# Linear attention, a softly gated mixture and a three-way max layer: banks from pools, the last layer's weights walked there and back, background work placed later

## The chip, the cores and the metric

One core of one Trainium2 chip runs the whole program in one launch. The metric is the device time of one execution in microseconds; the kernel before has a median of 1975.58 us over 3 runs (1972.33 to 1978.89).

## The reference

Three layers follow one another on 2304 tokens of 512 numbers. The first is attention with random features (4 batches, 8 heads, 576 tokens of 64). The second is a mixture of 8 experts, all of which see all tokens; its gate P is normalised by rows and columns eight times. The third takes the larger of three products and multiplies once more.

```
x   = attention(q, k, v, omega)                  # 2304 x 512
P   = exp(x @ w_gate - max); 8 times: P /= P.sum(1); P /= P.sum(0); P *= N / E
y   = sum over e of P[:, e] * (relu(x @ w1[e]) @ w2[e])      # 8 x (512 x 1024, 1024 x 512)
out = maximum(y @ m1, y @ m2, y @ m3) @ m_out                # 512 x 768 three times, 768 x 512
```

## The kernel before

**Tiles and stages.** The tokens are cut into three thirds of 768 and each layer is walked a third at a time, in phases 0 to 5. Phase 0 runs both layers of the mixture over the first third, phases 1 and 2 over the other two, and phases 3, 4 and 5 run the last layer over thirds one to three. A product of (768 tokens x 512) by (512 x 256) is computed by Winograd's scheme with seven products instead of eight. Its tokens' side is seven operands x0 to x6 (`x_operands`, stored in DRAM as xc1 to xc5 and loaded again by `load_x`), and its weights' side is seven operands made from w1 (`prepare_w1`) or from the last layer's weights (`last_weights`, stored as lc1 and lc2). Each number is split in a high and a low part, so that a product is six matmuls of 128x384 on PE (lines L401 to L403), all into one bank of the accumulator memory.

**A sub.** `sub_products` issues seven products into three kinds of banks: U (two banks in turn), V and W (one bank each). ACT copies U and V out as u1, u5 and u2 (L408), DVE adds them onto the other banks, and the four results go to ACT and DVE, which write h as a high part (ACT, L447 or L452) and a low part (DVE, L448 or L453). `tile_out` (L471 to L473) multiplies h by the second weights into one of four result banks, which DVE or ACT empties into acc (L484, L486). In phase 0 PE also runs one matmul for each of the eight gate rounds (L644), whose input cs DVE makes (L635 to L639 and L645 to L648); the gate begins with a maximum over all partitions on POOL (L630).

**The last layer.** A phase there has three turns of three subs. A sub's weights are seven pieces of 256 KB, loaded ahead into the tiles wa and wb in turn. The second weights of a turn are two pieces of 512 KB in w2_0 and w2_6 or w2_3 and w2_5. The seven operands of the next phase are loaded into x0 to x6 as their last readers in the phase before finish. The operands of phase 5 are computed in phase 3 into h0 to h5 and stored from there to xc5.

**What sets the order.** The attention is written out by hand. From there on, every step is a task with a cost, the keys that it reads and writes and the engines that may do it ("PD": POOL or DVE). `Tasks.ordered` (lines 41 to 149) plays the tasks through once: each engine takes, of the tasks that could start first, the one that is wanted earliest, and PE's tasks keep the order of the program. The instructions then stand on each engine in that order, and no engine passes over a waiting one. A load's time counts there as its bytes by a rate and a fixed part:

```python
return min(cost.values()) if on != "S" else 2000 + cost["S"]
```

All DMAs are issued by SP (`fetch`, L213), in one row, so a DMA whose tile is not yet free holds back those behind it. DVE and POOL additions go through one helper (`tt`, L210); so rows that read "L210" are of many places, and are told apart by their tiles. Names in the rows: g are raw weights or sums of them, w is w2_0 to w2_6, b is b11 to b22 and t is t1 to t4.

Of the kernel before, what the change touches and what calls it, by code (L numbers as in the profile page):

```python
# [23 lines left out]

FILL = 9
START = [("load", 0), ("squared", 0), ("squared", 1), ("norms", 0, 0), ("v", 1), ("load", 1), ("v", 0)]

# [13 lines left out]
class Tasks:  # L41
# [30 lines left out]
    def ordered(self):  # L72
# [24 lines left out]
        open_ = {e: set() for e in free}  # L97
        ready, port, wire = [0.0] * n, 0.0, 0.0
        best = dict.fromkeys(free)

        def choose(e):

            starts = []
            for i in open_[e]:
                t = max(free[e], ready[i])
                if e == "P" or e == "D" and tasks[i][4]:
                    t = max(t, port)
                starts.append((t, i))
            if not starts:
                return None  # L110
            t0 = min(starts)[0]
            return t0, min((wanted[i], i) for t, i in starts if t <= t0)[1], e
# [6 lines left out]
        for _ in range(n):  # L119
            for e in free:  # L120
                if best[e] is None:
                    best[e] = choose(e)
            start, i, e = min((b for b in best.values() if b), key=lambda b: (b[0], b[1]))
            order.append((i, e))
            for f in tasks[i][0]:
                open_[f].discard(i)
                best[f] = None
            cost = tasks[i][1][e]
            if e == "S":
                wire = max(wire, start) + cost  # L130
                free[e], end = start + 60, wire + 2000
            else:
                free[e] = start + cost
                end = free[e] + lag[e]
                if e == "P" or e == "D" and tasks[i][4]:
                    port = free[e]
                    best["P"] = best["D"] = None
            for j in after[i]:
                ready[j] = max(ready[j], free[e] if tasks[j][0] == e != "S" else end)
                left[j] -= 1  # L140
                if not left[j]:
                    for f in tasks[j][0]:
                        open_[f].add(j)
                        best[f] = None
# [4 lines left out]
def tile_performer__moe__max3(ctx, tc, kq_t, kq, v1, omega2, w_gate, w1, w2, m1, m2, m3, m_out, out):  # L149
# [49 lines left out]

    BANKS = [f"bank{k}" for k in range(8)]  # L200
    banks = {}

    def new_bank(k):
        return ps_m.tile([P, 512], F32, tag=k, name=k)

# [31 lines left out]
    def dma(kb, out, in_, r, w):  # L237
        return add("S", kb * 1024 / 350, lambda e: fetch(out(), in_()), r, w)

# [138 lines left out]
    u_turn = [0, 0, 1]  # L378
    U_BANKS, V_BANK, W_BANK = (BANKS[1], BANKS[0]), BANKS[2], BANKS[3]
    R_BANKS = BANKS[4:]  # L380
    r_turn = [0]

    def next_r():
        r_turn[0] += 1
        return R_BANKS[r_turn[0] % 4]

    def sub_products(k, before, results):

        ub = U_BANKS[u_turn.pop(0)]
        u_turn.append(1 - u_turn[-1])  # L390
        at = {"u": ub, "v": V_BANK, "w": W_BANK}

        def product(i, j, b, onto):
            before(i, j)
            kh, kl = w_keys(k, i)

            def run():
                ps, w, x = banks[b][:, :Q], ws[k][:, i].rearrange("p c (k f) -> p c k f", k=2), xo[j]
                given = dict(skip_group_check=onto)
                for c in range(2):  # L400
                    nc.tensor.matmul(ps, w[:, 0, c], x[:, c, 0], start=c == 0 and not onto, stop=False, **given)  # L401
                    nc.tensor.matmul(ps, w[:, 0, c], x[:, c, 1], start=False, stop=False, **given)  # L402
                    nc.tensor.matmul(ps, w[:, 1, c], x[:, c, 0], start=False, stop=c == 1, **given)  # L403

            pe(6 * 175, run, [*kh, *kl, (f"x{j}", 0), (f"x{j}", 1)], [b])

# [9 lines left out]
        to_u("u1", ub)  # L416
        product(*p[1], V_BANK, False)
        yield
        to_u("u5", V_BANK)
        product(*p[2], ub, True)  # L420
        yield
        to_u("u2", ub)
        product(*p[3], W_BANK, False)
        yield
        results(0, 0, W_BANK, lambda b, plus=plus: plus(W_BANK, W_BANK, "u1"), ("u1", W_BANK))
        product(*p[4], ub, True)
        yield
        results(1, 1, W_BANK, lambda b, plus=plus: plus(W_BANK, ub, "u5"), ("u5", ub))
        product(*p[5], V_BANK, True)
        yield  # L430
        results(0, 1, V_BANK, lambda b, plus=plus: plus(V_BANK, V_BANK, "u2"), ("u2", V_BANK))
        product(*p[6], ub, True)
# [122 lines left out]
    def h_parts(ks):  # L555
        return [(lambda k=k: t_(f"h{k}"), [(f"h{k}", 0)], [(f"h{k}", 1)]) for k in ks]

    def temps():
        return [(lambda k=k: t_(k), [k]) for k in ("b11", "b12", "b21", "b22", "t1", "t2")]
# [14 lines left out]

    def load_x(ph, j):
        for c in range(2):
            dma(384, lambda c=c: xo[j][:, c].bitcast(F32), lambda c=c: xc[ph][j][:, c], [("xc", ph, j, c)], [(f"x{j}", c)])

# [80 lines left out]
    def program():  # L659
# [19 lines left out]
        for s in range(SUBS):  # L679
# [175 lines left out]
        def max_results(m, parity):  # L855
# [17 lines left out]
            return results  # L873

        LAST = [("w2_0", "w2_6"), ("w2_3", "w2_5")]
        turn = 0
        for ph in (3, 4, 5):
            for n in range(3):
                parity = turn % 2
                tiles = LAST[parity]  # L880
                for m in range(3):
                    slot = (turn * 3 + m + 1) % 2

                    def before(i, j, n=n, m=m, slot=slot):
# [5 lines left out]
                    for i, _ in enumerate(sub_products(slot, before, max_results(m, parity))):  # L890
                        q = 7 * m + i
                        if len(queue) > 6:
                            take()
                        elif q >= 3 and q % 3 == 0 and not (ph == 3 and n == 0):
                            take()
                        elif ph == 3 and n == 0:
                            take()
# [8 lines left out]

                def weights(n=n, tiles=tiles):
                    for c, k in enumerate(tiles):
                        dma(512, lambda c=c, k=k: t_(k).bitcast(F32), lambda c=c: lc2[n][:, c], [("lc2", n)],
                            [(k, 0), (k, 1)])  # L910

                group = [lambda t=t, parity=parity, tiles=tiles, evict=evict: tile_out(t, parity, tiles, evict) for t in TILES]
                first = group[0]
                group[0] = lambda first=first, weights=weights: (weights(), first())
                queue += group
# [13 lines left out]
    def attention(pool, proj_pool):  # L929
# [3 lines left out]

        smalls.append(new_bank(BANKS[7]).rearrange("p (s j t h) -> p s j t h", s=2, j=2, t=128 // 2)[:, :, :, :TP])
        count = [0]
# [224 lines left out]
        def logits(s):  # L1160
# [10 lines left out]

            ps = new_bank(ring[(count[0] - 2) % 7]) if len(ring) == 7 else abank()
            for c in range(KD):
# [16 lines left out]
            def transposed():  # L1190
                ps = new_bank(ring[(count[0] - 2) % 7]) if len(ring) == 7 else abank()
                for j in range(n):
# [50 lines left out]

    smalls, ring = [], BANKS[:7]
    with tc.manual_schedule():
# [4 lines left out]
        with left as att:  # L1250
# [8 lines left out]
            ts.update({f"h{k}": a.tile([P, 2, Q], F32R, name=f"h{k}") for k in range(14)})  # L1259
            banks.update({k: new_bank(k) for k in BANKS[1:4]})  # L1260
            ring[:] = [BANKS[k] for k in (4, 5, 6, 0)]
            layers = feed_forward()
# [5 lines left out]
        while n < FILL:  # L1268
            next(layers)
            n += 1  # L1270
        banks.update({k: new_bank(k) for k in BANKS if k not in banks})
        b = ctx.enter_context(tc.tile_pool(name="b", bufs=1, side="left", reuse_waits="tile"))
# [62 lines left out]
```

## Time and profile before

| | |
|---|---|
| median of 3 runs | 1975.58 us (1972.33 to 1978.89) |
| the profiled execution | 1972.07 us, of which the span of the trace is 1970.1 |
| PE busy | 1888.4 us, 96% of the span |
| DVE, POOL, ACT busy | 75%, 50%, 40% |
| DMA | 579.49 MB, mean 294 GB/s |
| granted PE clock, mean of the span | 0.989 of full speed |

A row of a timeline begins with its start in us from the begin of the span and its duration; in square brackets stands the time for which its engine sat idle before it, and what ended that. "PEclk" is the granted clock as a share of the full one: 1.00 is 2.4 GHz and 0.50 is 1.2 GHz; a stretch with a value between holds some time at either. Phase 0 stands in the trace from about 196 us (its first products run beside the end of the attention), and phases 1 to 5 begin at about 735, 1190, 1690, 1754 and 1856 us.

### The profile page before, as it was taken

How to read it: one execution, taken by the hardware profiler on the slowest of the kernel's cores; microseconds unless marked ns; L12 is line 12 of the kernel's file. 1: busy time of each engine (PE TensorE's matmuls, PEld its weight loads, DVE VectorE, ACT ScalarE, POOL GpSimd, SP SyncE). 2: the span in 40 equal slices, each digit the busy share in tenths (PEclk: the TensorE clock that was granted, in tenths of full speed). 3: DMA queues.
4: the chain of work that ended last, by engine and by line, in shares of the span. 5: the costliest groups of instructions: out<-in, count | busy, mean ns of one | idle time of the engine just before them, and what ended most of it. 6: DMA issues, size and time to landing. Idle time of an engine off the chain costs nothing.

```text
span 1970.1 us, 33400 instructions
## 1 busy us (share of the span) xinstructions
PE 1888.4 (96%) x11521; PEld 1782.1 (90%) x11521; DVE 1481.7 (75%) x2694; ACT 796.4 (40%) x1805; POOL 984.9 (50%) x915
## 2 busy tenths in 40 slices
PE   7887899999999999999999999999999999989898
PEld 6666789878999999999999999999999999889897
DVE  6664798888878768988888888989886775633435
ACT  6665445545544435333333343433343332312221
POOL 4351577634455515686777775677764443300000
PEclk9999899999999999999999999999999999999999
DMA  6453789999988899899898898988998889987873
GB/s 213 159 151 131 273 279 386 372 347 332 339 317 300 315 341 352 328 330 316 316 312 311 307 335 285 319 316 294 312 387 290 259 249 352 355 314 218 301 236 117
DMA packets 282793, 579.49 MB, mean 294 GB/s; under 512 B 26528, under 2 KB 125568, under 8 KB 276992
## 3 DMA queue, kind: packets, MB, share of 16 engines
q1 hardware_dynamic: 282624, 577.35, 83.9%
q8 instruction: 92, 1.51, 0.3%
q14 instruction: 77, 0.63, 0.1%
HBM read 399.99 MB, written 177.26 MB: 293 GB/s over the span
## 4 chain that ended last, share of the span: by engine, by line
PE 85%; DVE 6%; DMA 4%; ACT 3%; issue 1%; POOL 1%; SPq 0%; DVEq 0%; POOLq 0%; ACTq 0%
PE bank L401 14%; PE bank L403 14%; PE bank L402 14%; PE bank L788 8%; PE bank L786 8%; PE bank L787 8%; PE bank L471 5%; PE bank L473 5%; PE bank L472 5%; PE bank L1023 2%; DMA x<-xc 2%; ACT qp L1046 1%; PE bank L956 1%; PE bank L1069 1%; ACT kp L1046 1%
## 5 line engine op out<-in xcount | busy, mean ns | idle before, releaser
L401 PE MATMUL bank<-x,wa 128*128 128x384 f32 x1302 | 441.1, 339 | 16.0 <-DVE bank L210 6.5
L403 PE MATMUL bank<-x,wa 128*128 128x384 f32 x1302 | 439.9, 338 | 9.5 <-DVE wa L210 9.5
L402 PE MATMUL bank<-x,wa 128*128 128x384 f32 x1302 | 438.7, 337 | 0.0
L408 ACT COPY u<-bank 128x384 f32<-128x384 f32 x369 | 176.9, 480 | 350.9 <-PE bank L403 348.0
L788 PE MATMUL bank<-h,w 128*128 128x384 f32 x896 | 303.2, 338 | 0.0
L786 PE MATMUL bank<-h,w 128*128 128x384 f32 x896 | 302.9, 338 | 0.0
L787 PE MATMUL bank<-h,w 128*128 128x384 f32 x896 | 301.9, 337 | 0.0
L210 DVE TENSOR_TENSOR acc<-bank,acc 128x384 f32<-128x384 f32 x420 | 231.4, 551 | 80.8 <-PE bank L788 79.4
L401 PEld LDWEIGHTS bank<-x,wa 128*128 128x128 f32 x1302 | 245.7, 189 | 27.2 <-DVE bank L210 7.6
L210 DVE TENSOR_TENSOR bank<-bank,u 128x384 f32<-128x384 f32 x342 | 191.9, 562 | 89.3 <-PE bank L403 83.2
L403 PEld LDWEIGHTS bank<-x,wa 128*128 128x128 f32 x1302 | 245.6, 189 | 11.4 <-DVE wa L210 11.1
L402 PEld LDWEIGHTS bank<-x,wa 128*128 128x128 f32 x1302 | 245.5, 189 | 5.0
L210 POOL TENSOR_TENSOR h<-b,h 128x384 fp32r<-128x384 f32 x144 | 155.7, 1090 | 143.4 <-ACT h L734 134.8
L210 POOL TENSOR_TENSOR h<-t,h 128x384 fp32r<-128x384 f32 x137 | 146.4, 1072 | 108.3 <-ACT h L734 94.3
L471 PE MATMUL bank<-w,h 128*128 128x512 f32 x492 | 195.2, 397 | 0.7 <-ACT h L452 0.7
L473 PE MATMUL bank<-w,h 128*128 128x512 f32 x492 | 194.5, 395 | 0.1
L472 PE MATMUL bank<-w,h 128*128 128x512 f32 x492 | 194.5, 395 | 0.0
L734 ACT CAST h<-b 128x384 fp32r<-128x384 f32 x192 | 98.3, 514 | 225.5 <-DVE b L749 208.5
L734 ACT CAST h<-t 128x384 fp32r<-128x384 f32 x256 | 127.5, 514 | 137.1 <-POOL t L210 109.6
L210 POOL TENSOR_TENSOR g<-g,g 128x256 f32<-128x256 f32 (+2 forms) x143 | 144.8, 1014 | 67.3 <-DVE g L210 30.7
L786 PEld LDWEIGHTS bank<-h,w 128*128 128x128 f32 x896 | 168.5, 188 | 0.0
L787 PEld LDWEIGHTS bank<-h,w 128*128 128x128 f32 x896 | 168.5, 188 | 0.0
(150 smaller groups left out, 3591.2 us busy)
## 6 DMA issues: line engine op xcount, KB each, us to landing
wa<-wc SPq DMA_DIRECT2D x441, 256.0 KB, 5.1
w<-wc SPq DMA_DIRECT2D x217, 512.0 KB, 5.7
g<-in_moe_w_dram SPq DMA_DIRECT2D x82, 512.0 KB, 7.4
wc<-w SPq DMA_DIRECT2D x64, 512.0 KB, 7.0
wc<-wa SPq DMA_DIRECT2D x16, 1792.0 KB, 8.6
wc<-wb SPq DMA_DIRECT2D x16, 1792.0 KB, 7.4
x<-xc SPq DMA_DIRECT2D x70, 384.0 KB, 7.5
wb<-lc SPq DMA_DIRECT2D x98, 256.0 KB, 4.7
```

The costliest lines, as they stand in the source:

```text
L210: (nc.gpsimd if on == "P" else nc.vector).tensor_tensor(out=out, in0=in0, in1=in1, op=op)
L401: nc.tensor.matmul(ps, w[:, 0, c], x[:, c, 0], start=c == 0 and not onto, stop=False, **given)
L402: nc.tensor.matmul(ps, w[:, 0, c], x[:, c, 1], start=False, stop=False, **given)
L403: nc.tensor.matmul(ps, w[:, 1, c], x[:, c, 0], start=False, stop=c == 1, **given)
L408: act(Q, lambda: nc.scalar.copy(t_(n), banks[b][:, :Q]), [b], [n])
L471: nc.tensor.matmul(ps, h[:, 0, c], t_(wh)[:, part], start=f == 0, stop=False)
L472: nc.tensor.matmul(ps, h[:, 0, c], t_(wl)[:, part], start=False, stop=False)
L473: nc.tensor.matmul(ps, h[:, 1, c], t_(wh)[:, part], start=False, stop=f == 1)
L734: act(Q, lambda: nc.scalar.copy(t_(h)[:, 0], t_(n)), [n], [(h, 0)])
L786: nc.tensor.matmul(ps, wv[:, 0, sub, d], h[:, 0], start=o == 0, stop=False)
L787: nc.tensor.matmul(ps, wv[:, 0, sub, d], h[:, 1], start=False, stop=False)
L788: nc.tensor.matmul(ps, wv[:, 1, sub, d], h[:, 0], start=False, stop=o == 1)
```

## The change

Five things change.

1. The accumulator's eight banks are taken from three pools, "ph" (4), "po" (3) and "small" (1), instead of by fixed numbers. When the attention ends, U0, V0 and W are the three of "po", U1, V1 and two result banks the four of "ph", and the third result bank is "small". So V has two banks, which take turns with U's, and results have three banks instead of four.
2. The planner counts a load as 3.5 us (instead of 2) beside its bytes, and its rate as 340 (instead of 350). DVE is not offered a task that POOL could do as well before 6 us ahead of when it is wanted; that wanted time is moved by how late PE runs in the plan.
3. The last layer's phase 4 walks its weights backwards (groups 2, 1, 0), and phases 3 and 5 forwards. So the weights of the first two subs of phases 4 and 5 are still in wa and wb and are not loaded (2 x 14 pieces of 256 KB).
4. In phase 4 the operands x0, x3 and x4 are read from h0 to h5, into which they are loaded during phase 3; x1, x2, x5 and x6 stay in their tiles. So x0, x3 and x4 of phase 5 are loaded into their own tiles before phase 4.
5. The operands of phase 5 (xc5) are made in w2_1, w2_2 and w2_4 instead of h0 to h5. The operands for phases 1 and 2 are put in the program after subs 8 and 16 instead of 3 and 12.

```diff
+SLACK = 6000
...
-            return min(cost.values()) if on != "S" else 2000 + cost["S"]
+            return min(cost.values()) if on != "S" else 3500 + cost["S"]
...
             for i in open_[e]:
                 t = max(free[e], ready[i])
+                if e == "D" and tasks[i][0] == "PD" and wanted[i] + late > t + SLACK:
+                    continue
...
+            if e == "T":
+                late = start - nominal[i]
+                best["D"] = None
...
-    def new_bank(k):
-        return ps_m.tile([P, 512], F32, tag=k, name=k)
+    def new_bank(tag):
+        return ps_m.tile([P, 512], F32, tag=tag, name=tag, bufs={"ph": 4, "po": 3, "small": 1}[tag])
...
-        ub = U_BANKS[u_turn.pop(0)]
+        xs = xs or x_home
+        n = u_turn.pop(0)
         u_turn.append(1 - u_turn[-1])
-        at = {"u": ub, "v": V_BANK, "w": W_BANK}
+        ub, vb, wb = f"bu{n}", f"bv{n}", "bw"
...
+    def x_beside(j, c):
+
+        if j not in (0, 3, 4):
+            return x_home(j, c)
+        h = f"h{2 * (0, 3, 4).index(j) + c}"
+        return lambda: t_(h), [(h, 0), (h, 1)]
...
-            if s == 3:
+            if s == 8:
                 x_operands(1, temps(), h_parts(range(6)))
-            if s == 12:
+            if s == 16:
                 x_operands(2, temps(), h_parts(range(6)))
...
         for ph in (3, 4, 5):
+            back = ph == 4
+            xs = x_beside if back else x_home
             for n in range(3):
                 parity = turn % 2
                 tiles = LAST[parity]
+                group = 2 - n if back else n
                 for m in range(3):
-                    slot = (turn * 3 + m + 1) % 2
-
-                    def before(i, j, n=n, m=m, slot=slot):
+                    a = 3 * n + m
+                    slot = (a + 1) % 2
+                    mat = 8 - a if back else a
+
+                    def before(i, j, a=a, slot=slot, mat=mat):
                         kh, kl = w_keys(slot, i)
-                        dma(256, lambda: ws[slot][:, i].bitcast(F32), lambda: lc1[3 * n + m][:, i], [("lc1", 3 * n + m)], kh + kl)
-                        if n == 0 and m == 0:
-                            load_x(ph, j)
+                        if ph == 3 or a > 1:
+                            dma(256, lambda: ws[slot][:, i].bitcast(F32), lambda: lc1[mat][:, i], [("lc1", mat)], kh + kl)
+                        if a == 0:
+                            load_x(ph, j, xs)
...
                 if ph == 3 and n == 1:
-                    x_operands(5, g_pieces(), h_parts(range(6)))
+                    x_operands(5, g_pieces(), w2_parts((1, 2, 4)))
...
-            ring[:] = [BANKS[k] for k in (4, 5, 6, 0)]
+            banks.update({k: new_bank("po") for k in ("bu0", "bv0", "bw")})
+            ring[:] = ["ph"]
...
+        banks.update({k: new_bank("ph") for k in ("bu1", "bv1", "r0", "r1")})
+        banks["r2"] = new_bank("small")
```

Where the planner puts things is seen in the order of each engine. First POOL where phase 0 begins, around the maximum over the partitions. The rows without operands (ISA) set POOL up for another kind of work, the row with mx is the maximum itself; g and w2 belong to the preparation of weights. Before:

```order
L210 TENSOR_TENSOR w2_1_2536<-g1_82,w2_0_2535 128x512
L210 TENSOR_TENSOR wb_2531<-g3_84,wb_2531 128x2x256
L210 TENSOR_TENSOR g4_85<-g1_82 128x256
L630 ISA
L630 ISA mx_68<-mx_68 128x1
L210 ISA
L210 TENSOR_TENSOR w2_3_2779<-g0_81,w2_2_2778 128x512 x2
L210 TENSOR_TENSOR w2_5_2781<-g4_85,w2_4_2780 128x512
L210 TENSOR_TENSOR g4_85<-g0_81 128x256
```

And POOL at the same place now:

```order
L215 TENSOR_TENSOR wb_2531<-g3_84,wb_2531 128x2x256
L215 TENSOR_TENSOR w2_1_2536<-g1_82,w2_0_2535 128x512
L215 TENSOR_TENSOR w2_5_2777<-g4_85,w2_4_2776 128x512
L652 ISA
L652 ISA mx_68<-mx_68 128x1
L215 ISA
L215 TENSOR_TENSOR w2_3_2775<-g0_81,w2_2_2774 128x512
L215 TENSOR_TENSOR g3_84<-g1_82 128x256 x2
L215 TENSOR_TENSOR g3_84<-g1_82,g3_84 128x256
L215 TENSOR_TENSOR wa_79<-g3_84,wa_79 128x2x256
```

An addition for w2_5 now stands ahead of the first of the two calls; behind the second, sums g3 for the weights wa of the next sub have come to POOL from DVE, which did them before.

Second, SP between phases 3 and 4: x0 to x6 are the operands' tiles, xc4 and xc5 the stores they are loaded from, lc1 and lc2 the weights. Before:

```order
L213 DMA wb_2531<-lc1_1_145 128x512
L213 DMA x4_76<-xc4_94 128x768 x2
L213 DMA wb_2531<-lc1_1_145 128x512
L213 DMA x1_73<-xc4_94 128x768 x2
L213 DMA wb_2531<-lc1_1_145 128x512
L213 DMA x5_77<-xc4_94 128x768 x2
L213 DMA wb_2531<-lc1_1_145 128x512
L213 DMA w2_3_2779<-lc2_0_153 128x1024
L213 DMA w2_5_2781<-lc2_0_153 128x1024
L213 DMA x2_74<-xc4_94 128x768 x2
L213 DMA wb_2531<-lc1_1_145 128x512
L213 DMA x6_78<-xc4_94 128x768 x2
```

And SP at the same place now:

```order
L218 DMA xc5_95<-w2_4_2776 128x768
L218 DMA x0_72<-xc5_95 128x768 x2
L218 DMA x3_75<-xc5_95 128x768
L218 DMA xc5_95<-w2_1_2536 128x768
L218 DMA x3_75<-xc5_95 128x768
L218 DMA x4_76<-xc5_95 128x768
L218 DMA xc5_95<-w2_2_2774 128x768
L218 DMA x1_73<-xc4_94 128x768 x2
L218 DMA x5_77<-xc4_94 128x768 x2
L218 DMA w2_3_2775<-lc2_2_155 128x1024
L218 DMA w2_5_2777<-lc2_2_155 128x1024
L218 DMA x2_74<-xc4_94 128x768 x2
```

The weights and x0, x3, x4 of phase 4 are gone from here, and x0, x3, x4 of phase 5 and the last stores to xc5 have come.

Third, SP between phases 4 and 5. Before:

```order
L213 DMA wa_79<-lc1_1_145 128x512
L213 DMA x4_76<-xc5_95 128x768 x2
L213 DMA wa_79<-lc1_1_145 128x512
L213 DMA x1_73<-xc5_95 128x768 x2
L213 DMA wa_79<-lc1_1_145 128x512
L213 DMA x5_77<-xc5_95 128x768 x2
L213 DMA wa_79<-lc1_1_145 128x512
L213 DMA w2_0_2535<-lc2_0_153 128x1024
L213 DMA w2_6_2782<-lc2_0_153 128x1024
L213 DMA x2_74<-xc5_95 128x768 x2
```

And now:

```order
L218 DMA wb_2531<-lc1_0_144 128x512 x7
L218 DMA x1_73<-xc5_95 128x768 x2
L218 DMA x5_77<-xc5_95 128x768 x2
L218 DMA w2_0_2535<-lc2_0_153 128x1024
L218 DMA w2_6_2778<-lc2_0_153 128x1024
L218 DMA x2_74<-xc5_95 128x768 x2
L218 DMA x6_78<-xc5_95 128x768 x2
L218 DMA wb_2531<-lc1_2_146 128x512 x4
```

Here only x1, x5, x2 and x6 and the two pieces of second weights are left; the loads of x0, x3, x4 and of wa are gone.

## Rows read from the trace of the kernel before

**Rows 1.** The page's first part: busy time and share of each engine.
```profile
PE 1888.4 (96%) x11521; PEld 1782.1 (90%) x11521; DVE 1481.7 (75%) x2694; ACT 796.4 (40%) x1805; POOL 984.9 (50%) x915
```
**Rows 2.** Chain that ended last: share of the span by engine.
```profile
PE 85%; DVE 6%; DMA 4%; ACT 3%; issue 1%; POOL 1%; SPq 0%; DVEq 0%; POOLq 0%; ACTq 0%
```
**Rows 3.** Busy time by stage: stretch, length, busy us by engine, clock, DMA share, GB/s.
```profile
196.00:470.00 274.00, 256.42 (x1236) 225.89 (x1233) 229.05 (x423) 133.12 (x275) 160.56 (x157) 0.97 0.92 332
...
735.00:1190.00 455.00, 454.44 (x2599) 453.42 (x2598) 404.36 (x677) 173.02 (x367) 329.09 (x298) 1.00 0.92 323
...
1690.00:1970.00 280.00, 261.55 (x1335) 240.57 (x1334) 124.95 (x224) 70.53 (x147) 8.21 (x8) 0.97 0.75 256
```
**Rows 4.** Timeline of POOL, 183 to 212 us.
```profile
184.05 1.27 POOL L210 TENSOR_TENSOR w<-g,w 128x512 fp32r<-128x512 f32 x1 [3.48 <-ACT w L207]
...
186.53 0.73 POOL L210 TENSOR_TENSOR g<-g 128x256 f32<-128x256 f32 x1
198.79 0.38 POOL L630 PARTITION_ALL_REDUCE mx<-mx  x1 [11.54 <-DVE mx L629]
209.29 3.74 POOL L210 TENSOR_TENSOR w<-g,w 128x512 fp32r<-128x512 f32 x3 [10.12 <-DMA wc<-w]
```
**Rows 5.** Timeline of ACT, 196 to 211 us.
```profile
198.69 1.14 ACT L207 CAST w<-g 128x512 fp32r<-128x512 f32 x2
```
**Rows 6.** Timeline of DVE, 205 to 222 us.
```profile
213.86 0.42 DVE L210 TENSOR_TENSOR g<-g,g 128x256 f32<-128x256 f32 x1 [7.62 <-POOL g L210]
```
**Rows 7.** Timeline of PE, in phase 0.
```profile
217.42 0.69 PE L403 MATMUL bank<-x,wa 128*128 128x384 f32 x1 [6.35 <-DVE wa L210]
...
219.50 0.52 PE L403 MATMUL bank<-x,wa 128*128 128x384 f32 x1
...
242.25 0.60 PE L644 MATMUL bank<-cs,ones 128*128 128x8 f32 x2 [3.31 <-DVE cs L639]
```
**Rows 8.** Short stretches, columns as in rows 3.
```profile
222.00:275.00 53.00, 47.72 (x225) 41.10 (x224) 47.99 (x103) 20.20 (x42) 42.02 (x43) 0.94 0.74 265
275.00:470.00 195.00, 189.54 (x925) 167.89 (x924) 167.00 (x285) 98.51 (x203) 112.79 (x109) 0.99 0.98 356
...
1763.00:1774.00 11.00, 7.65 (x24) 6.33 (x25) 1.25 (x2) 0.48 (x1) 0.00 (x0) 0.69 0.94 356
1865.00:1874.00 9.00, 6.70 (x21) 5.59 (x22) 0.84 (x2) 0.48 (x1) 0.00 (x0) 0.62 1.04 395
```
**Rows 9.** PE's waits from 196 to 470 us: us in total, times, longest.
```profile
PE bank L403 <- DVE wa L210: 9.5, 4, 6.4
PE bank L644 <- DVE cs L639: 4.6, 2, 3.3
```
**Rows 10.** The page's DMA issues: KB each, median us to landing.
```profile
g<-in_moe_w_dram SPq DMA_DIRECT2D x82, 512.0 KB, 7.4
```
**Rows 11.** PE's waits from 1702 us to the end.
```profile
PE bank L401 <- DMA x<-xc: 8.4, 5, 3.5
PE bank L401 <- DVE h L453: 4.0, 7, 0.6
```
**Rows 12.** Timeline of PE, where phases 4 and 5 begin.
```profile
1765.25 0.44 PE L401 MATMUL bank<-x,wa 128*128 128x384 f32 x1 [3.43 <-DMA x<-xc]
...
1767.98 0.66 PE L401 MATMUL bank<-x,wa 128*128 128x384 f32 x1 [0.91 <-DMA x<-xc]
...
1866.89 0.69 PE L401 MATMUL bank<-x,wb 128*128 128x384 f32 x1 [3.48 <-DMA x<-xc]
...
1869.61 0.66 PE L401 MATMUL bank<-x,wb 128*128 128x384 f32 x1 [0.41 <-DMA x<-xc]
```
**Rows 13.** Timeline of SP, where phase 5 begins: the loads of x1.
```profile
1852.10 0.96 SPq L213 DMA_DIRECT2D x<-xc  x2
```
**Rows 14.** What writes or reads xc, 1690 to 1760 us: stores of xc5, time to landing.
```profile
L213 SPq DMA_DIRECT2D xc<-h x14: 319/454/917, 1692.2 to 1716.2; - x14
...
DMA to landing us min/median/max: 3.1/5.9/7.8
```

More of the change, by code (lines that the diff above doesn't have):

```diff
@@ L97, in ordered @@
         open_ = {e: set() for e in free}
-        ready, port, wire = [0.0] * n, 0.0, 0.0
+        ready, port, wire, late = [0.0] * n, 0.0, 0.0, 0.0
         best = dict.fromkeys(free)
@@ L130, in ordered @@
                 wire = max(wire, start) + cost
-                free[e], end = start + 60, wire + 2000
+                free[e], end = start + 60, wire + 3500
             else:
@@ L237, in dma @@
     def dma(kb, out, in_, r, w):
-        return add("S", kb * 1024 / 350, lambda e: fetch(out(), in_()), r, w)
+        return add("S", kb * 1024 / 340, lambda e: fetch(out(), in_()), r, w)
     def pe(ns, run, r, w):
@@ L397, in run @@
             def run():
-                ps, w, x = banks[b][:, :Q], ws[k][:, i].rearrange("p c (k f) -> p c k f", k=2), xo[j]
+                ps, w, x = banks[b][:, :Q], ws[k][:, i].rearrange("p c (k f) -> p c k f", k=2), [xs(j, c)[0]() for c in range(2)]
                 given = dict(skip_group_check=onto)
                 for c in range(2):
[L401 to L405, printed above, removed]
+                    nc.tensor.matmul(ps, w[:, 0, c], x[c][:, 0], start=c == 0 and not onto, stop=False, **given)
+                    nc.tensor.matmul(ps, w[:, 0, c], x[c][:, 1], start=False, stop=False, **given)
+                    nc.tensor.matmul(ps, w[:, 1, c], x[c][:, 0], start=False, stop=c == 1, **given)
+            pe(6 * 175, run, [*kh, *kl, *xs(j, 0)[1], *xs(j, 1)[1]], [b])
         def to_u(n, b):
@@ L416, in sub_products @@
         to_u("u1", ub)
-        product(*p[1], V_BANK, False)
+        product(*p[1], vb, False)
         yield
-        to_u("u5", V_BANK)
+        to_u("u5", vb)
         product(*p[2], ub, True)
@@ L556, in h_parts, with w2_parts @@
         return [(lambda k=k: t_(f"h{k}"), [(f"h{k}", 0)], [(f"h{k}", 1)]) for k in ks]
+    def w2_parts(ks):
+        return [
+            (lambda k=k: t_(f"w2_{k}")[:, : 2 * Q].rearrange("p (c q) -> p c q", c=2), [(f"w2_{k}", 0)], [(f"w2_{k}", 0), (f"w2_{k}", 1)])
+            for k in ks
+        ]
     def temps():
@@ L880, in program @@
                 tiles = LAST[parity]
+                group = 2 - n if back else n
                 for m in range(3):
-                    slot = (turn * 3 + m + 1) % 2
-                    def before(i, j, n=n, m=m, slot=slot):
+                    a = 3 * n + m
+                    slot = (a + 1) % 2
+                    mat = 8 - a if back else a
+                    def before(i, j, a=a, slot=slot, mat=mat):
                         kh, kl = w_keys(slot, i)
-                        dma(256, lambda: ws[slot][:, i].bitcast(F32), lambda: lc1[3 * n + m][:, i], [("lc1", 3 * n + m)], kh + kl)
-                        if n == 0 and m == 0:
-                            load_x(ph, j)
-                    for i, _ in enumerate(sub_products(slot, before, max_results(m, parity))):
-                        q = 7 * m + i
[L892 to L896, printed above, removed]
+                        if ph == 3 or a > 1:
+                            dma(256, lambda: ws[slot][:, i].bitcast(F32), lambda: lc1[mat][:, i], [("lc1", mat)], kh + kl)
+                        if a == 0:
+                            load_x(ph, j, xs)
+                    for i, _ in enumerate(sub_products(slot, before, max_results(m, parity), xs)):
+                        q = 7 * m + i
+                        if len(queue) > 6 or ph == 3 and n == 0 or q >= 3 and q % 3 == 0:
                             take()
@@ L905, in evict, with weights @@
                         dma(256, lambda: out[r0 : r0 + P, :], lambda: a_of(t), acc_keys(t * DM, (t + 1) * DM), [("out", r0)])
-                def weights(n=n, tiles=tiles):
+                def weights(group=group, tiles=tiles):
                     for c, k in enumerate(tiles):
[L909 to L915, printed above, removed]
+                        dma(512, lambda c=c, k=k: t_(k).bitcast(F32), lambda c=c: lc2[group][:, c], [("lc2", group)], [(k, 0), (k, 1)])
+                items = [lambda t=t, parity=parity, tiles=tiles, evict=evict: tile_out(t, parity, tiles, evict) for t in TILES]
+                first = items[0]
+                items[0] = lambda first=first, weights=weights: (weights(), first())
+                queue += items
                 if ph == 3 and n == 1:
-                    x_operands(5, g_pieces(), h_parts(range(6)))
+                    x_operands(5, g_pieces(), w2_parts((1, 2, 4)))
                 turn += 1
@@ L1242, in attention @@
             done.pop()()
-    smalls, ring = [], BANKS[:7]
+    smalls, ring = [], ["ph", "po", "po", "po", "ph", "ph", "ph"]
     with tc.manual_schedule():
```

32 lines of the change are left out of this document (15 added, 17 removed).

## The prediction

> **What bounds the kernel now.** I read the page's busy times first: PE is busy for 1888.4 us, 96% of the span, and the next engine, DVE, for 75% [rows 1]. The chain that ended last agrees, with 85% of the span on PE [rows 2]. The change leaves PE's matmuls and their order alone, so what it can move is PE's idle time, 1970.1 - 1888.4 = 82 us, and the stretches at the lower clock that follow a wait. Then I read the busy time by stage to see where the idle time lies [rows 3]: 274 - 256.4 = 17.6 us between 196 and 470 us, 0.6 us in phase 1, and 280 - 261.6 = 18.4 us in the last layer. The rest, some 45 us, lies nearly all in the attention, whose instructions stay as they are and whose banks rotate in the same turn but for the gate's logits; I give it nothing, with 1 us to either side. So two places decide: phase 0 and the last layer.
>
> **The last layer: V in two banks.** PE waits there seven times, up to 0.6 us each and 4.0 us together, for a low part of h (L453) [rows 11]. These are first products into V of a turn, whose bank the turn before still empties. With two banks the product goes into the other one, which was emptied a sub earlier, and the next thing late is W, needed three products on, some 3 us at 1.05 us a product. So the 4.0 us go. Bounds: 0 to 4.0; I take -4.0.
>
> **Results in three banks.** A result bank is wanted again one product and one eviction earlier. Neither list of PE's waits has a row for one that is not empty, and phase 1, where each product of the second layer takes one, has PE busy for 454.4 of 455 us [rows 3, 9, 11]. The cover is that slack, which I can't size in a row; I take +0.5, with 0 to +3.
>
> **Phase 4 to 5.** PE waits 3.48 + 0.41 us for x2 and x6 [rows 12]. Then the granted clock is 0.62 over 9 us [rows 8]: (1 - 0.62) / 0.5 x 9 = 6.8 us at 1.2 GHz, of which PE idles about 1.5, so the rest loses 5.3 / 2 = 2.7 us. SP had 14 loads of x and 14 of weights to issue there, and now has 8 of x, of 0.39 MB, and the two of 0.52 MB: 4.2 MB, at 395 GB/s [rows 8] 10.6 us. x1 could be issued at 1852.1, as before [rows 13], by the time its reader is done; x6 then lands at about 1863 to 1865, its landing time included. PE wants x2 at 1866.89 - 3.48 = 1863.4 and x6 a product later. That is a wait of 0 to 1 us in place of 3.9, which I take to leave the clock up; if it falls all the same, some 3 us of the gain stay. I take -6.6, with bounds -6.6 and 0.
>
> **Phase 3 to 4.** Here the wait is 3.43 + 0.19 + 0.91 = 4.5 us, and the clock 0.69 over 11 us, again 6.8 us at the lower level [rows 8, 12]. Six loads of x and 14 of weights leave the queue, but six loads of x for phase 5 and the last stores to xc5 enter it ahead of x1, so the bytes ahead of x2 are about 7 MB as before. The stores now come from three buffers instead of six. A store lands after 5.9 us, up to 7.8 [rows 14]; with a cast of about 0.5 and an addition on POOL of about 1 us, a buffer comes round in some 8 us, and 14 operands in three buffers take 14 / 3 x 8 = 37 us, where 24 us passed between the first and the last store before [rows 14]. Starting later than 1692, they end about where phase 4 starts. Two things are queued behind: the cast for w2_1 on ACT waits for a landing ahead of the copies u1 and u2 of phase 3's last sub, for whose bank PE waits; and the last store on SP waits for its addition ahead of x1. Each can hold PE for 2 or 3 us, but what PE loses there it does not wait again for x2. I take +1.5, with 0 to +5.
>
> **Phase 0: POOL's two loads in series.** Before, POOL idles 11.54 us ahead of the maximum over partitions, until its input from DVE is there, then runs it for 0.38 us, and idles 10.12 us behind it [rows 4]. The second idle time is put down to a DMA; but the addition's other input, the cast on ACT, was done by about 199.3 [rows 5], and by the order only one of the two calls without operands, which set up POOL for another kind of work, stands between. I read 10.1 us as the price of such a call, and call it a load. The first one was hidden in the 11.54 us, so its price lies between 0 and 11.5. DVE then waits 7.62 us for a sum from POOL [rows 6], and PE 6.35 for wa [rows 7].
>
> Now w2_5 stands ahead of the first load. Its cast is ready at about 199.3 to 199.8 [rows 5] and the addition takes 1.27 [rows 4], so the load starts near 200.8. With 10.1 us for it the maximum is over at 211.2 and the second load at 221.3. Behind it: 1.27 for w2_3, two sums at 0.73 [rows 4], 0.42 on DVE [rows 6], a cast of 0.6, then a sum of 0.73 and the addition of 1.27 for wa, part of it beside the cast: PE's matmul that stood at 219.50 [rows 7] starts at about 221.3 + 1.27 + 1.46 + 0.73 + 1.27 = 226.0, or 6.5 us later. Behind the waiting DVE instruction, which takes the maximum, stand the low part of h and the additions for wa, and behind these ACT's copies, so PE loses this in two waits and is back at the lower clock after each, as before after one.
>
> The Trainium skill, "GPSIMD Engine Reference", section "2.1 Instruction dispatch", says that the first call to a freshly loaded routine pays about 6 us that no instruction shows. The trace's gap of 10.12 us has the same form and is longer; the measurement decides. By the page's 6 us for each load the same matmul would start at 226.0 - 2 x 4.1 = 217.8, 1.7 us earlier than before, and the whole sum below would come out 5 us lower, given what the gate takes back.
>
> Some of the 6.5 us is given back at the gate's second matmul, for which PE waited 3.31 us at 242.25, with a clock of 0.94 over 53 us behind, which is 6.4 us at half speed and 3.2 us of work [rows 7, 8]. DVE has fewer of the early additions for x1 and x2 in front of cs now. If cs is there by 245.4, nothing is waited for, the clock stays up, and 6.5 - 3.3 - 3.2 = 0 is left. If cs is as late behind the first matmul as before, 6.5 stays. I take +1.
>
> Then come the waits for wa and wb of each sub. 9.5 - 6.4 = 3.1 us of those on wa lie behind the first [rows 9], and from 275 to 470 us PE idles 195 - 189.5 = 5.5 us [rows 8]. The planner gives DVE such work no more than 6 us ahead, and 18 additions go to POOL, where one of 512 takes 1.27 us [rows 4]. A load of 512 KB lands after 7.4 us [rows 10], where the planner now counts 3.5 + 1.5 = 5.0. So the cover is thinner: 2.4 us late in 6 of slack. Bounds -5 (all of it goes) to +14; near the row of 5.5 I take +2.
>
> **The sum.** -4.0 + 0.5 - 6.6 + 1.5 + 1 + 2 = -5.6 us. Against the profiled execution that is 1972.07 - 5.6 = 1966.5; the median of the runs shown lies 3.5 above it, so I put the forecast at 1975.58 - 5.6 = 1970.0. A measurement here can tell about 0.3% from no change, 5.9 us; the forecast stands near that bound.
>
> **Rivals.** First, DVE held back too long. Phase 0 has 24 subs from the eighth on, and each needs its wa or wb at its first product. If a late load and POOL's turn cost each of them 0.7 us, that is 17 us instead of 2: 1970.0 + 15 = 1985, slower. For it speaks the landing of 7.4 us, and DVE's 229 of 274 us busy, which leaves little room to catch up [rows 3, 10]; against it, that POOL has 113 us free there. It decides from 15 us of new waits in phase 0; then the last layer's gain no longer pays.
>
> Second, POOL's first load costs little, because the routine is found loaded or is fetched early: the matmul at 219.50 comes 3.6 us earlier, the gate's wait goes too, and the early stretch gains about 6 where I have +3. The time is 1970 - 9 = 1961. For it: no row shows what the first load cost. Against: the second cost 10.1 us.
>
> Third, the walk there and back does not do what it says: x2 or x6 still come late in phase 5, or phase 4's longer queue takes it back (+5), and 4.0 for V is all that is left: about -1 to +1, 1975. For it: from x1's release to x6 there are only about 11 us, and the 4.2 MB take 10.6.
>
> **Chances.** The forecast's case (-2 to -9 us) 0.42, late preparation 0.20, the cheap load 0.18, the walk that gains nothing 0.20. Faster by more than 5.9 us holds about half of the first and nearly all of the third of these, and some of the rest: 0.40. Slower by more than 5.9 us is most of the second and a little of the last: 0.20. That leaves 0.40 between. The forecast alone would have 1966 to 1975; to leave out no more than 2 in 10 the range goes from 1958 to 1984.
>
> **What would show it.** V's waits gone from PE's list; no wait above 1 us and no half clock where phase 5 begins, and still some 4 us or more where phase 4 begins. On POOL an idle time of some 10 us on both sides of the maximum, and PE's wait behind it ending near 226. I am wrong if POOL idles for less than 5 us before the maximum and after w2_5, if phase 5 begins with a wait above 2 us, or if PE's waits for wa and wb between 230 and 470 us exceed 15 us.

## The result, and the profile after

The changed kernel takes 1947.01 us (median of 4 runs, 1944.3 to 1949.24) against 1976.9 us before (4 runs), a ratio of 0.985 with a 95% interval of 0.983 to 0.987. That is 29.9 us faster, outside the range of the prediction. The profiled execution took 1947.44 us, 24.6 less than the profiled one of before.

The page's first part, as in [rows 1]: PE's busy time hardly moves, and POOL has 25 us more.

```profile
PE 1881.6 (97%) x11521; PEld 1778.9 (91%) x11521; DVE 1482.3 (76%) x2676; ACT 796.9 (41%) x1805; POOL 1010.1 (52%) x933
```

The busy times by stage, columns as in [rows 3]. Phases 1 to 5 begin 10 to 17 us earlier now, so the stretches don't hold quite the same work.

```profile
0.00:196.00 196.00, 172.51 (x2314) 144.10 (x2314) 134.39 (x396) 136.92 (x438) 82.90 (x66) 0.94 0.59 194
196.00:470.00 274.00, 248.06 (x1171) 216.39 (x1171) 227.04 (x397) 123.08 (x252) 160.42 (x158) 0.96 0.89 322
...
1690.00:1945.00 255.00, 246.76 (x1282) 229.82 (x1280) 112.30 (x201) 67.23 (x140) 21.89 (x22) 0.99 0.69 231
```

Up to 196 us PE does 2314 matmuls, where it did 2202; from there to 470 us it idles for 25.9 us, where it idled for 17.6. In the last layer 8.2 us of idle time are left of 18.4.

Both programs issue the same 11,521 matmuls, so the n-th of one can be set against the n-th of the other. The table gives the start of a matmul in each profiled run less its start before, in us: near the first product of the feed-forward (the 2050th), near 503 us before (the 3600th, phase 0's second half), near 1656 us before (the 10,000th) and the last. Runs without a range in the last column were profiled and timed once; the kernel before stood at 1976.6 to 1977.9 us beside them. The profiled run of before, at 1972.07 us, is faster than these, so the shifts at the last matmul show some 5 to 6 us less of a gain than the times do.

| kernel | 2050th | 3600th | 10,000th | last | time, us |
|---|---|---|---|---|---|
| changed | -33.5 | -10.0 | -9.7 | -24.3 | 1947.0 (1944.3 to 1949.2) |
| before, attention's pools alone (e1) | -33.9 | -31.2 | -31.3 | -31.0 | 1941.0 |
| e1 and two V banks (e9) | -33.5 | -28.6 | -30.1 | -35.7 | 1936.0 |
| changed, attention in a fixed turn (e3) | +4.8 | +27.3 | +27.6 | +12.3 | 1984.0 |
| changed, old planner (e2) | -34.0 | -28.9 | -30.3 | -45.7 | 1927.1 |
| changed, DVE not held back (e7) | -34.6 | -16.8 | -14.4 | -28.7 | 1943.2 |
| changed, old price of a load (e8) | -34.8 | -28.3 | -30.6 | -47.6 | 1924.0 |
| changed, a load at 2.75 us | -34.6 | -18.6 | -20.0 | -33.4 | 1938.3 |
| changed, a load at 5 us | -33.4 | -11.8 | -13.0 | -28.9 | 1942.9 |
| changed, operands held back (e6) | -32.8 | -32.4 | -25.8 | -39.9 | 1931.7 |
| e2 with row maximum (e11) | -33.9 | -37.2 | -40.7 | -57.4 | 1914.4 |
| e8 with row maximum (e13) | -33.7 | -36.3 | -38.6 | -56.2 | 1916.3 (1915.4 to 1917.5) |
| e13, operands held back (e14) | -33.7 | -44.6 | -47.4 | -63.7 | 1909.0 (1906.3 to 1912.6) |

So the change gains 33.5 us in the attention, gives 23.5 back in phase 0, and gains 14.6 in the last layer.

The attention is where the prediction saw nothing. PE's waits between 14 and 170 us before (columns as in [rows 9]):

```profile
PE bank L1023 <- ACT kp L1046: 17.6, 14, 1.4
PE bank L1023 <- ACT qp L1046: 7.6, 13, 0.6
PE bank L1093 <- ACT qp L1046: 2.8, 14, 0.2
```

And PE's waits between 14 and 136 us in the changed kernel:

```profile
PE po L1117 <- ACT qp L1070: 3.3, 13, 0.6
PE po L1097 <- ACT rem L1070: 0.8, 1, 0.8
```

The first product of a pair of heads, in two turns that follow each other, on PE before:

```profile
36.87 0.38 PE L1023 MATMUL bank<-om,raw 64*128 64x128 f32 x2 [1.30 <-ACT kp L1046]
...
42.67 1.16 PE L1023 MATMUL bank<-om,raw 64*128 64x128 f32 x16 [0.58 <-ACT qp L1046]
...
45.35 0.49 PE L1023 MATMUL bank<-om,raw 64*128 64x128 f32 x2
47.14 0.38 PE L1023 MATMUL bank<-om,raw 64*128 64x128 f32 x2 [1.30 <-ACT kp L1046]
```

And in the changed kernel:

```profile
37.80 0.38 PE L1047 MATMUL ph<-om,raw 64*128 64x128 f32 x2
...
40.48 0.37 PE L1047 MATMUL po<-om,raw 64*128 64x128 f32 x1
...
40.70 0.27 PE L1047 MATMUL po<-om,raw 64*128 64x128 f32 x1
...
45.65 0.38 PE L1047 MATMUL ph<-om,raw 64*128 64x128 f32 x2
```

A turn takes 7.85 us instead of 10.27, and 14 of them make 33.9. Of these 2.42 us a turn, 1.88 are the idle times of the two waits (1.30 and 0.58). The rest is time in which matmuls beside a wait don't overlap their neighbours: before, 1.79 us lie between the start of the projection's first two matmuls and the next, of which 1.30 are idle, and now the next start 0.22 us behind them. The projections (L1023) went into banks whose last projection ACT was still reading, for the exponentials of kp and qp. A turn takes 14 banks, two rounds of the ring of seven, so every product met the same bank in every turn. By the waits of the built program, a pool does not go round in a fixed turn: it hands out the bank that was given back first. There the second bank of the projection no longer waits for ACT's exponentials but for ACT's copy of a transposed block, which is long done.

### The profile page after: what moved, and what is told of

Read it like the earlier page. It is cut to its first block, busy times and chain, and to the rows that moved or that the text cites. A ratio compares the mean times of both kernels' runs of the same rounds, so it can differ in the third digit from the quotient of the medians.

```text
span 1945.7 us, 33270 instructions
## 1 busy us (share of the span) xinstructions
PE 1881.6 (97%) x11521; PEld 1778.9 (91%) x11521; DVE 1482.3 (76%) x2676; ACT 796.9 (41%) x1805; POOL 1010.1 (52%) x933
## 4 chain that ended last, share of the span: by engine, by line
PE 87%; DVE 6%; DMA 3%; ACT 2%; issue 1%; POOL 1%; SPq 0%; DVEq 0%; ACTq 0%
PE po L406 8%; PE po L408 8%; PE po L407 8%; PE ph L408 6%; PE ph L406 6%; PE ph L407 6%; PE ph L810 5%; PE ph L808 5%; PE ph L809 5%; PE ph L476 3%; PE ph L478 3%; PE ph L477 3%; PE small L810 3%; PE small L808 3%; PE small L809 3%; PE small L478 2%
## 5 line engine op out<-in xcount | busy, mean ns | idle before, releaser
L406 PE MATMUL po<-x,wa 128*128 128x384 f32 x676 | 227.3, 336 | 4.0 <-DVE po L215 2.3
L407 PE MATMUL po<-x,wa 128*128 128x384 f32 x676 | 226.9, 336 | 0.0
L408 PE MATMUL po<-x,wa 128*128 128x384 f32 x676 | 226.8, 336 | 0.0
L406 PE MATMUL ph<-x,wa 128*128 128x384 f32 x588 | 199.6, 339 | 12.1 <-ACT wa L212 7.4
L408 PE MATMUL ph<-x,wa 128*128 128x384 f32 x588 | 199.7, 340 | 3.8 <-DVE wa L215 3.5
L810 PE MATMUL ph<-h,w 128*128 128x384 f32 x598 | 202.5, 339 | 0.0
L808 PE MATMUL ph<-h,w 128*128 128x384 f32 x598 | 202.3, 338 | 0.0
L809 PE MATMUL ph<-h,w 128*128 128x384 f32 x598 | 201.6, 337 | 0.0
L407 PE MATMUL ph<-x,wa 128*128 128x384 f32 x588 | 198.9, 338 | 0.0
L215 DVE TENSOR_TENSOR po<-po,u 128x384 f32<-128x384 f32 x230 | 129.0, 561 | 89.5 <-PE po L408 86.2
L215 DVE TENSOR_TENSOR acc<-ph,acc 128x384 f32<-128x384 f32 x280 | 154.0, 551 | 52.6 <-PE ph L810 51.6
L413 ACT COPY u<-po 128x384 f32<-128x384 f32 x186 | 89.4, 482 | 182.1 <-PE po L408 178.6
L215 POOL TENSOR_TENSOR wb<-g,wb 128x512 fp32r<-128x512 f32 (+2 forms) x101 | 126.7, 1263 | 56.7 <-ACT wb L212 50.3
L413 ACT COPY u<-ph 128x384 f32<-128x384 f32 x183 | 88.0, 481 | 152.6 <-PE ph L408 151.2
L406 PEld LDWEIGHTS po<-x,wa 128*128 128x128 f32 x676 | 127.0, 188 | 6.8 <-DVE po L215 3.0
L476 PE MATMUL ph<-w,h 128*128 128x512 f32 x328 | 131.4, 401 | 0.0
```

Source lines behind the costliest of these rows:

```text
L215: (nc.gpsimd if on == "P" else nc.vector).tensor_tensor(out=out, in0=in0, in1=in1, op=op)
L406: nc.tensor.matmul(ps, w[:, 0, c], x[c][:, 0], start=c == 0 and not onto, stop=False, **given)
L407: nc.tensor.matmul(ps, w[:, 0, c], x[c][:, 1], start=False, stop=False, **given)
L408: nc.tensor.matmul(ps, w[:, 1, c], x[c][:, 0], start=False, stop=c == 1, **given)
L413: act(Q, lambda: nc.scalar.copy(t_(n), banks[b][:, :Q]), [b], [n])
L476: nc.tensor.matmul(ps, h[:, 0, c], t_(wh)[:, part], start=f == 0, stop=False)
```

## The experiments

**The attention's pools alone (e1), and the fixed turn put back (e3).** e1 is the kernel before with these edits in the main, and with the names of the pools wherever a bank is taken; e3 undoes them in the changed kernel.

```diff
-        return ps_m.tile([P, 512], F32, tag=k, name=k)
+        return ps_m.tile([P, 512], F32, tag=tag, name=tag, bufs={"ph": 4, "po": 3, "small": 1}[tag])
...
-    smalls, ring = [], BANKS[:7]
+    smalls, ring = [], ["ph", "po", "po", "po", "ph", "ph", "ph"]
```

> The kernel before with one part of the change: the attention takes its banks from the pools (4, 3 and 1); planner, feed-forward banks (one V, four results) and last layer stay as before. Theory A (the pools alone speed up the attention, since a bank is handed on in the order in which banks come free and no longer in a fixed turn): PE's waits of 1.3 us for kp and 0.6 us for qp vanish from all 14 turns, a turn takes 7.85 us instead of 10.28, and the first feed-forward product starts at 141.4 us instead of 174.9. Rival: the attention's gain comes from something else in the change; then the product starts at 174 to 175 us. For phase 0 it tells two theories apart. Catch-up (the preparation of weights has its own pace, so PE that comes 33 us early waits for it): of the 33 us only 8 to 14 are left at 470 us. Planner (the new rules cause phase 0's waits): 25 to 33 us are left at 470 us. Time by catch-up 1958 to 1966, by planner 1940 to 1948.

> The changed kernel with the attention's banks in the fixed turn of before (ring of seven); the feed-forward banks, the planner and the last layer as changed. Theory A: the first feed-forward product starts at 174.5 to 175 us again. Catch-up: phase 0 then loses little, 3 us or less against before where the change loses 23.5, so at 470 us it stands within 4 us of before, and the time is 1955 to 1963 (the last layer's 14.7 us are kept). Planner: phase 0 loses 15 us or more all the same and the time is 1970 or more.

e1: the feed-forward starts 33.9 us earlier, and at the end 31.0 are left, 1941.0 us: less than the whole change. So the attention's gain is the pools', and it lasts to the end; that phase 0 catches up by itself is refuted. e3: the waits are back to the tenth.

```profile
PE bank L1049 <- ACT kp L1072: 17.6, 14, 1.4
PE bank L1049 <- ACT qp L1072: 7.6, 13, 0.6
```

Its attention is 4.8 us longer than in the profiled run of before with the same waits, which I had not expected; the clock was 0.95 up to 174 us, where it was 0.99 before. Phase 0 then loses 22.5 us, much as in the changed kernel. e3 at 1984.0 is the change without its pools: 6.1 us slower than the kernel before on the same chip, in one run of each; what the clock did in the attention of that run of before isn't recorded.

**The planner's rules (e2, e7, e8).** e2 takes both back, e7 only the holding back of DVE, e8 only the price of a load.

```diff
-                if e == "D" and tasks[i][0] == "PD" and wanted[i] + late > t + SLACK:
-                    continue
...
-            return min(cost.values()) if on != "S" else 3500 + cost["S"]
+            return min(cost.values()) if on != "S" else 2000 + cost["S"]
...
-        return add("S", kb * 1024 / 340, lambda e: fetch(out(), in_()), r, w)
+        return add("S", kb * 1024 / 350, lambda e: fetch(out(), in_()), r, w)
```

> The changed kernel with the planner's old rules: DVE is not held back, a load counts 2 us and 350 instead of 3.5 us and 340. Catch-up: phase 0 loses 20 to 27 us as in the changed kernel (23.5), and the time stays at 1944 to 1952. Planner: phase 0 loses only 5 to 12 us, and the time falls to 1928 to 1938.

> The changed kernel without the rule that holds DVE back; loads still count 3.5 us and 340. The old rules as a whole bring phase 0 back by about 19 us and the time to 1927. If the holding back alone causes the lost time: phase 0 loses 3 to 8 us, and the time is 1925 to 1932. If the longer load time causes it: phase 0 loses 18 us or more and the time stays at 1942 to 1950. If both are needed, between, 1933 to 1941.

> The changed kernel with a load's old price in the plan (2 us and 350); DVE is still held back. The complement of the run without holding back. If the holding back causes the lost time: 1942 to 1950. If the load time causes it: 1925 to 1932. If both are needed to do harm: both runs lie near 1930.

Phase 0 (from the 2050th to the 3600th matmul) loses 23.5 us in the changed kernel, 5.1 in e2, 17.8 in e7 and 6.5 in e8. So without the higher price of a load most of the loss is gone, and the holding back, which I had blamed in the first rival, does little harm with the old price: e8's one run is 3.1 us below e2's, which is less than the 4.9 us between the runs of the changed kernel. e2's time lies 0.9 us below the range expected for the planner's rules. That the price does not act alone is seen in e6 below. PE's waits from 190 to 470 us in the changed kernel:

```profile
PE po L408 <- DVE wb L215: 6.5, 5, 2.8
PE small L666 <- DVE cs L661: 5.7, 2, 3.9
PE ph L408 <- DVE wa L215: 3.5, 4, 1.4
PE ph L666 <- DVE cs L661: 3.1, 3, 1.3
PE po L406 <- ACT wb L212: 2.6, 3, 1.2
PE ph L406 <- ACT wa L212: 2.2, 1, 2.2
PE po L406 <- ACT u L413: 1.2, 1, 1.2
PE po L408 <- POOL wb L215: 1.2, 2, 0.7
```

And in e8, where these four are all that the view has:

```profile
PE ph L408 <- DVE wa L215: 4.9, 3, 2.8
PE small L666 <- DVE cs L661: 3.2, 1, 3.2
PE ph L406 <- ACT wa L212: 3.0, 3, 1.2
PE ph L666 <- DVE cs L661: 2.7, 1, 2.7
```

The waits for wa and wb, 16.0 us in the first list, are 7.9 here, and those for cs go from 8.8 to 5.9.

**The price of a load, at two more values.** Only the number 3500 is changed, to 2750 and to 5000.

> The changed kernel with a load counted at 2.75 us in the plan (2 us with rate 350 gave 1924, 3.5 us with rate 340 gave 1947). If a higher price makes the plan issue the raw weights later before their use, step by step: 1930 to 1940, with leads from issue to first use of 13 to 17 us for the subs 7 to 15 of phase 0 (16 to 20 before, 11 to 15 in the changed kernel). If the bad order at 3.5 is one unlucky plan: the time lies outside that, at 1926 or less or at 1945 or more.

> The changed kernel with a load counted at 5 us in the plan. Step by step: more lost in phase 0 than the 23.5 us at 3.5 us, and 1952 to 1975 in all. One unlucky plan at 3.5: 1940 or less.

At 2.75 us phase 0 loses 16.0 us, and the mean lead from a raw load's issue to PE's first use of its weights, over subs 7 to 15, is 14.6 us, both as expected step by step (before it is 15.0 on average; 16 to 20 holds for the first four of these subs alone). But 7.5 of these 16.0 us are lost up to the 2300th matmul, around POOL's maximum; behind it it is 8.5, where e8 loses 5.4 and the changed kernel 21.2. At 5 us it loses 21.6, no more than at 3.5, and 1942.9 lies in neither range. So each of the three prices above 2 us costs 14 to 23 us in all against e8, but not the more the higher it is. The lead alone doesn't tell it either: it is 13.1 us in the changed kernel, and 17.9 in e7, which loses 17.8 us all the same, mostly on wb. By which step of the plan the higher price turns into late weights stays open, and each of these figures is one plan and one run.

**V in two banks (e9).** e1 with V's second bank and three result banks.

```diff
-    U_BANKS, V_BANK, W_BANK = (BANKS[1], BANKS[0]), BANKS[2], BANKS[3]
-    R_BANKS = BANKS[4:]
+    U_BANKS, V_BANKS, W_BANK = (BANKS[1], BANKS[0]), (BANKS[2], BANKS[4]), BANKS[3]
+    R_BANKS = BANKS[5:]
```

> The kernel with the attention's pools alone (1941.0), and with it two banks for V and three for results; planner and last layer's walk as before. By the prediction the seven waits of 0.55 to 0.6 us behind the low part of h go, 4.0 us, and three result banks cost 0.5: 1936 to 1938. If three banks for results cost as much as V gains: 1940 to 1942. What the last layer gains beyond this (14.7 us in the changed kernel) is then the walk's.

1936.0, as expected. In the last layer it gains 5.6 us, e1 loses 0.3; phase 0 is 2.2 us worse than in e1, in a plan that came out differently. In e1 the view of PE's waits of the last layer has the row for V, and in e9 it has none.

```profile
PE po L401 <- DVE h L453: 3.9, 7, 0.6
```

What e2 gains there beyond e9, 15.4 - 5.6 = 9.8 us, comes with the walk and with items 4 and 5 of the change; no run takes these apart.

**POOL's maximum and its loads (e11).** In e2 each token's row gets the maximum over its partition; the row normalisation cancels the difference.

```diff
-        add("P", 3000, lambda e: nc.gpsimd.partition_all_reduce(mx[:, 1:2], mx[:, 0:1], P, bass.bass_isa.ReduceOp.max), ["mx0"], ["mx1"])
-        dve(lambda: nc.vector.tensor_scalar_mul(mx[:, 1:2], mx[:, 1:2], -1.0), [], ["mx1"])
+        dve(lambda: nc.vector.tensor_scalar_mul(mx[:, 1:2], mx[:, 0:1], -1.0), ["mx0"], ["mx1"])
```

> The changed kernel with the planner's old rules, where the gate subtracts each token row's maximum over the partition instead of the one over all partitions (the row normalisation cancels the difference), so that POOL's call and its two loads are gone. If POOL's second load is what PE waits for behind the maximum (6.3 us, and the clock behind it): that wait falls below 1 us, and the time from 1927 to 1918 to 1923. If POOL's load is hidden by other late work (DVE, casts): the wait stays at 4 us or more, and the time within 2 us of 1927.

1914.4, more than expected. e2's only wait of PE from 165 to 200 us is gone in e11, whose view of that stretch is empty:

```profile
PE ph L406 <- DVE wa L213: 6.3, 1, 6.3
```

**The operands held back (e6), and the gains together (e13, e14).** The operands of phases 1 and 2 may not be computed before PE has done what stands ahead of subs 8 and 16.

```diff
+                hold[0] = tasks.last
                 x_operands(1, temps(), h_parts(range(6)))
+                hold[0] = None
```

> The changed kernel, where the operands of phase 1 may not be computed before PE has finished what stands ahead of sub 8, and those of phase 2 not before sub 16 (they have been done from 170 to 372 us). If DVE and POOL's work on these operands is what makes the weights late in phase 0: the waits for wa, wb and cs between 190 and 310 us (about 12 us of idle time) fall to 6 or less, and the time falls by 4 to 10 us, to 1937 to 1943. If the weights are late for another reason (their loads, the order within a sub): the time stays within 3 us of 1947.

> The changed kernel with the old price of a load (2 us, 350; DVE still held back) and the row maximum in place of POOL's maximum over partitions. If the two gains are of different waits and add up: 1924 - 13 = 1911, and 1907 to 1916 as a range. If phase 0 then waits for the weights all the same: 1918 to 1924.

> As the run with old price and row maximum, and the operands of phases 1 and 2 held back until sub 8 and sub 16. On the changed kernel this brought 15 us. If that was because it relieved the same lateness as the price of a load does: within 4 us of the run without holding back, 1907 to 1915. If it is a gain of its own: 1896 to 1903.

e6 is 15 us faster than the changed kernel, more than the 4 to 10 expected: phase 0 loses 0.4 us up to the 3600th matmul, and 6.6 are lost behind it. So the work on these operands does stand in the way of the weights, and the price of 3.5 us, which e6 keeps, does its harm, in these runs, only where that work may come early: in the changed kernel ACT's casts for it run from 171 to 372 us, in e6 from 323 us on. With the old price and without POOL's call the holding back still brings 7.3 us: the time lies in the first of the two ranges expected, while the gain is more than the 4 us set for it. e13 at 1916.3 is just above its range and not faster than e11, so there the holding back of DVE gains nothing. e14 is the best version: 1909.0 us, 0.966 of before (0.964 to 0.967), 38 us faster than the changed kernel.

## Why the prediction was wrong

**The attention (0 ± 1; measured -33.5).** This is the step that failed: "whose instructions stay as they are and whose banks rotate in the same turn but for the gate's logits; I give it nothing". The instructions stay, but a pool hands out banks by their return, and e1 and e3 show that the pools alone make the 33 us. The waits on kp and qp were in the trace, 25 us in two rows; I took it that nothing in the change touched them.

**The last layer (-9.1 without the 0.5 for results; measured -14.6).** V's term was -4.0 and the result banks' +0.5; e9 against e1 gives -5.9 for both. Phase 4 to 5 was right: PE waits 0.69 us for x2, and 1.0 us together with the wait behind it, where 0 to 1 was predicted, and the clock stays at 2.4 GHz, as these rows show (PE's first wait, and the stretch around it, as in [rows 12] and [rows 8]).

```profile
1846.79 0.44 PE L406 MATMUL ph<-x,wb 128*128 128x384 f32 x1 [0.69 <-DMA x<-xc]
```

```profile
1843.00:1852.00 9.00, 7.91 (x38) 6.42 (x37) 3.05 (x5) 0.48 (x1) 0.00 (x0) 1.00 1.01 385
```

Between the 10,850th and the 11,100th matmul, which hold it and one wait for V of 0.6 us, 5.7 us are gained, where -6.6 was forecast for the walk alone. Phase 3 to 4 had the wrong sign: +1.5 forecast, while between the 10,350th and the 10,600th matmul 3.9 us are gained, two of V's waits (1.1 us) among them. The wait for x2 is shorter and one behind DVE's writing of b has come (PE where phase 4 begins), and the clock falls as before.

```profile
1750.36 0.66 PE L406 MATMUL po<-x,wb 128*128 128x384 f32 x1 [2.21 <-DMA x<-xc]
...
1753.36 0.66 PE L406 MATMUL po<-x,wb 128*128 128x384 f32 x1 [0.70 <-DVE b L215]
```

```profile
1746.00:1759.00 13.00, 10.09 (x37) 8.32 (x36) 2.81 (x5) 0.53 (x2) 0.00 (x0) 0.74 0.94 358
```

The stores from three buffers take 41 us, where I had worked out 37, but the last is issued at 1735.8 us, 5.6 us before phase 4's first matmul, and ACT's casts wait for them 0.7 us in all. The rows are what writes or reads xc from 1670 to 1745 us, as in [rows 14].

```profile
L218 SPq DMA_DIRECT2D xc<-w x14: 319/382/1693, 1694.5 to 1735.8; - x14
...
  ACT w L535: 0.7, 1
```

**POOL's two loads (10.1 us each; measured 6.2 and 7.0).** They do stand in series on both sides of the maximum (POOL in the changed kernel, as in [rows 4]).

```profile
167.34 1.32 POOL L215 TENSOR_TENSOR w<-g,w 128x512 fp32r<-128x512 f32 x1 [13.96 <-ACT w L212]
174.82 0.38 POOL L652 PARTITION_ALL_REDUCE mx<-mx  x1 [6.16 <-issue]
182.14 1.25 POOL L215 TENSOR_TENSOR w<-g,w 128x512 fp32r<-128x512 f32 x1 [6.95 <-issue]
```

The figure of about 6 us in the Trainium skill, "GPSIMD Engine Reference", section "2.1 Instruction dispatch", which I set aside for the gap of 10.12 us, lies near what these two rows show, 6.16 and 6.95 us. PE's wait behind it is 5.22 us, where 6.35 stood before; the chain to the 2300th matmul costs 2.3 us of the 33.5, where the forecast had +6.5 there and +1 after the gate. The price of the whole call depends on the plan: 12.7 us in e2's (e11), 7.7 in e8's (1924.0 to 1916.3, e13).

**The weights of phase 0 (+2, up to +14; measured +21.2).** From the 2300th to the 3600th matmul the shift falls from -31.2 to -10.0. PE idles 15.2 us more there than before (25.9 against 10.7); most of the rest is matmuls at the lower clock, which the trace shows for 20 us there, where it was 10. The first rival had the place and the engine that PE waits for, and its size, 17 us, was somewhat low; the sign that I gave, more than 15 us of waits for wa and wb from 230 us on, came with 16.0. But it blamed the holding back, and e7, e8 and e6 show the price of a load, together with the early work on the operands. The result was faster all the same, since no case had the 33.5 us in it. Without the pools the time is 1984.0 (e3, one run), near the rival's 1985, in part by chance: phase 0 loses more than the rival says, and the last layer gains more.

## What to carry to other kernels

Where buffers are handed out, ask by which rule, before and after: a pool that gives the buffer returned first can take away waits that a ring of fixed turn repeats in each round, and the rows that such waits fill (here 14 times 1.3 and 0.6 us) belong in the sum as soon as a change touches how buffers are named. A planner's cost is not better for lying nearer to the measured one: 3.5 us for a load is nearer to the trace than 2 us, and costs 17 us of phase 0 in this plan. When a change has several parts, the total can hide a part that loses; run each alone.

## What the runs showed of the hardware

POOL's idle time behind the maximum has two sizes: 6.9 to 8.3 us in the six kernels where the call ahead of the maximum was paid just before it, and 10.1 to 10.7 us in the five where that call lay hidden in an earlier idle time of 11.5 to 13.3 us. I don't know why the second then costs 3 us more. The clock in the attention isn't the same from run to run with the same waits: 0.95 in e3 against 0.99 before, up to 174 us, where e3 is 4.8 us later. In e3 the clock is 0.83 in four stretches of 10 us (from 20, 80, 130 and 140 us), before in one (from 120 us). In the two profiled runs whose attention has lost these waits, the changed kernel and e1, it is 1.00 in every stretch from 20 to 140 us.
